# Chunk-selected attention with a gated FFN: units of half a batch for all eight heads, and scores of four heads in row tiles

## The chip, the cores and the metric

The kernel runs on one core of a Trainium2 chip. The metric is the device time in microseconds (us). All comparisons use runs of the same ("fast") state: a run more than 1.5% above the fastest of the same kernel is left out, also from the medians quoted. The kernel before takes 394.27 us (median of 4 runs, 393.13 to 394.62).

Names of the engines in the profile: PE is the matrix engine, PEld its weight loads, DVE the vector engine, ACT the scalar engine, POOL the general engine that also issues the weights' transfers here, and SP the engine that issues the other transfers. PSUM is the memory into which the matmuls of these kernels write, in banks. A row tile is a product that takes only 32 or 64 of the 128 rows of PE, a column tile one that takes only some of its columns; several of them can run side by side.

## The reference

Four batches, eight heads, 768 positions, 64 features per head. Keys lie in 24 chunks of 32. For each query an upper bound of each chunk's scores is computed, and only keys in the six chunks with the largest bounds take part in the attention. The attention's output goes through an FFN with a sigmoid gate (512 to 1536 to 512).

```
k_min, k_max = min and max of the keys of each chunk of 32
ub = sum(maximum(q * k_min, q * k_max), -1)          # per query and chunk
ub = where(causal by chunk, ub, -1e9)
top_chunks = argsort(ub)[..., -6:]
scores = q @ k.T / 8, -1e9 where the chunk isn't chosen or the key is later
attn = softmax(scores) @ v
x = attn, heads side by side                        # 3072 x 512
out = (sigmoid(x @ w_gate) * (x @ w_val)) @ w_out
```

The choice of chunks compares bounds, so these are kept in fp32. Scores, values and FFN use fp16 operands.

## The kernel before

A group is four heads of one batch; there are eight groups. A group's keys are loaded twice, by rows and by chunks (`kc`). The mask of a query is appended to its 64 features as 32 further rows, and so one matmul of 96 rows gives the masked scores of a head. The bounds are one product of 128 rows per head: `[max; -min]` of the chunks against `[relu(q); relu(-q)]`.

```python
nc.sync.dma_start(d["kc"], k[b, h0:h0 + 4].rearrange("h (c s) d -> (h c) s d", s=CH))
...
def chunk_bounds(g):                       # two reduces of 96 x 2048, strided
    nc.vector.tensor_reduce(kmm[:, 0:64], kv, AX.X, ALU.max)
    nc.vector.tensor_reduce(kmm[:, 64:128], kv, AX.X, ALU.min, negate=True)
...
def bounds(g):
    for x in range(2):
        for h in range(4):                 # K = 128, four heads in four column tiles
            nc.tensor.matmul(ps[32 * h:32 * h + 32, x, 0:hw], kcat[g % 2][:, h, :],
                             d[("qcat", h)][:, hw * x:hw * x + hw], start=True, stop=True)
...
def score(g, h, x):                        # one head, one PSUM bank
    hk, hq = headK[4 * (g % 2) + h], headQ[4 * (g % 2) + h]      # [96, 768] each
    ...
    for (jb, i0, w) in banks[x]:
        nc.tensor.matmul(ps[:, o:o + w], hk[:, 128 * jb:128 * jb + 128], hq[:, i0:i0 + w],
                         start=True, stop=True)
        o += w
    nc.scalar.activation(at[:, b0:b0 + n], ps, AF.Exp, scale=scale)
...
def ffn_tasks(b):                          # the FFN waits for a whole batch
    for t0 in range(0, S, TCH):            # two halves of 384 tokens
        ...  12 gate and value products, then 3 outputs
```

The attention of group g, the preparation of group g+1 and the FFN of the batch before are interleaved. The layer that records the kernel reorders each engine's instructions by its own estimate of time, so the built order differs from the source; and each engine then takes its own list in order (e13 below shows PE waiting 5 us for that).

The softmax here doesn't subtract the row's maximum and nothing guards it: scores larger than these inputs give would overflow.

## Time and profile before

| before (profiled span 393.6 us) | |
|---|---|
| PE busy | 320.2 us (81%) |
| first matmul of an FFN output | 136.6 us |
| a batch in the steady part | 82.7 us |
| FFN of the last batch, alone at the end | about 47 us |

First the page of the kernel before: the span, the busy time of each engine with its number of instructions, then the busy tenths of PE and its granted clock in forty slices of the span, then a queue with packets, MB and share.

```profile
span 393.6 us, 6906 instructions
PE 320.2 (81%) x2696; PEld 197.2 (50%) x2696; DVE 230.0 (58%) x486; ACT 204.6 (52%) x393; POOL 73.5 (19%) x77
...
PE   1071549287598999799979998799999999999996
PEclk9996557856969999999999999999999999999999
...
q1 hardware_dynamic: 79616, 31.47, 37.3%
```

A slice is 9.8 us. In the first twelve slices PE has gaps and its clock falls to half; from the thirteenth PE is nearly full. So the kernel has two stages with different limits: a start that waits for inputs, DVE and ACT, and a steady part that is bound by PE.

The chain of waits of the kernel before, with start, duration and what ran, shows the steady rhythm by the first output matmuls of each half batch:

```profile
136.57 2.60 PE o_0_0_1471 L296 x12
...
178.90 2.61 PE o_384_0_2048 L296 x12
...
261.58 2.61 PE o_384_0_3203 L296 x12
```

From 178.90 to 261.58 is one batch, 82.7 us.

The timeline of PE of the kernel before, first where scores pass into gate products, then at the bounds (start, duration, line, output<-inputs, sizes; the durations are longer than the steps because matmuls are pipelined, so read the starts):

```profile
232.26 0.39 PE L243 MATMUL sc_0_0_2792<-hq_132,hk_131 96*128 96x128 f16 x4
232.49 0.38 PE L243 MATMUL sc_0_1_2798<-hq_132,hk_131 96*128 96x128 f16 x3
232.71 0.33 PE L281 MATMUL g_384_0_2804<-xT_0_1456,wg_145 128*128 128x384 f16 x1
...
251.93 0.33 PE L287 MATMUL v_384_7_3041<-xT_3_2194,wv_146 128*128 128x384 f16 x1
252.19 0.46 PE L169 MATMUL ubT_3023<-qcat_0_2859,kcat_139 128*32 128x320 f32 x1
...
252.48 0.43 PE L169 MATMUL ubT_3023<-qcat_0_2859,kcat_139 128*32 128x320 f32 x1
```

Four score blocks of 128 queries, mask included, take 232.26 to 232.49: 0.057 us each. A gate matmul of 384 columns takes 0.16. The value matmul at 251.93 hands over to the bounds 0.26 us later, 0.1 us more than its usual step: a change of the tile shape from 128x128 to 128x32 costs about that. Each fp32 product of the bounds shows as two passes.

### The profile page before, as it was taken

The numbers are of one execution on the slowest core, as the hardware profiler recorded it, in microseconds if no ns is written. First come the engines' busy times: TensorE is split into PE (matmuls) and PEld (weight loads), VectorE is DVE, ScalarE is ACT, GpSimd is POOL, SyncE is SP. The second block draws the span as 40 slices with busy tenths as digits, with TensorE's granted clock in tenths as the row PEclk, the third lists the DMA queues.
The fourth block names the chain that finished last, engine by engine and source line by source line (L and its number), as shares of the span: only waits on it lengthen the run. The fifth ranks groups of instructions, "written<-read, shape, count | busy, mean of one in ns | idle before, by whom it ended". The sixth has DMA issues, their size and how long they took to land.

```text
span 393.6 us, 6906 instructions
## 1 busy us (share of the span) xinstructions
PE 320.2 (81%) x2696; PEld 197.2 (50%) x2696; DVE 230.0 (58%) x486; ACT 204.6 (52%) x393; POOL 73.5 (19%) x77
## 2 busy tenths in 40 slices
PE   1071549287598999799979998799999999999996
PEld 0040335164464656455645555465666566565552
DVE  4947629967949745855596658664556544142230
ACT  1150446266576548555556656655876466332331
POOL 4504143232312051003300230011101001000000
PEclk9996557856969999999999999999999999999999
DMA  9999999297920964433615010002000100100102
GB/s 181 217 214 214 208 212 195 66 217 148 214 62 15 226 156 108 101 62 86 155 42 120 28 55 0 2 2 80 2 2 27 55 2 1 55 27 28 54 2 80
DMA packets 84400, 36.62 MB, mean 93 GB/s; under 512 B 75920, under 2 KB 80528, under 8 KB 83600
## 3 DMA queue, kind: packets, MB, share of 16 engines
q1 hardware_dynamic: 79616, 31.47, 37.3%
q0 software_dynamic: 4752, 4.72, 7.2%
q8 instruction: 21, 0.34, 0.4%
q14 instruction: 11, 0.09, 0.1%
HBM read 34.60 MB, written 6.29 MB: 104 GB/s over the span
## 4 chain that ended last, share of the span: by engine, by line
PE 58%; DVE 17%; ACT 8%; issue 6%; SPq 5%; DMA 4%; POOL 1%; ACTq 0%; DVEq 0%; POOLq 0%
SPq L125 5%; DMA k_177<-in_k_dram 3%; DMA kc_151<-in_k_dram 2%; DVE kmm_1096 L140 1%; DVE kmm_209 L140 1%; DVE kmm_721 L141 1%; DVE kmm_1096 L141 1%; DVE kmm_209 L141 1%; PE o_0_0_2626 L296 1%; PE o_0_0_3781 L296 1%; PE o_384_0_3203 L296 1%; PE o_384_0_2048 L296 1%; PE o_0_0_1471 L296 1%; PE o_384_2_4783 L296 1%; PE o_384_1_4298 L296 1%
## 5 line engine op out<-in xcount | busy, mean ns | idle before, releaser
L287 PEld LDWEIGHTS <-wv_146 128*128 128x128 f16 x384 | 37.9, 99 | 28.3 <-issue 4.2
L281 PEld LDWEIGHTS <-wg_145 128*128 128x128 f16 x384 | 35.7, 99 | 23.2 <-issue 6.7
L153 PE MATMUL qT_0_212<-ident_103,q_148 128*128 128x128 f32 x5 | 1.3, 426 | 8.4 <-DMA q_148<-in_q_dram 8.4
L243 PEld LDWEIGHTS <-hk_123 96*128 96x128 f16 x48 | 4.8, 122 | 3.8 <-issue 2.9
L153 PE MATMUL qT_1_227<-ident_103,q_148 128*128 128x128 f32 x5 | 1.3, 427 | 5.9 <-DVE qcat_1_221 L160 5.9
L153 PE MATMUL qT_0_369<-ident_103,q_176 128*128 128x128 f32 x5 | 1.3, 426 | 5.8 <-DMA q_176<-in_q_dram 5.8
L140 DVE TENSOR_REDUCE kmm_1096<-kc_1044 96x64 f32<-96x2048 f32 x1 | 3.7, 3667 | 3.7 <-PE kct_756 L146 3.7
L272 PE MATMUL xps_1_671<-ident_108,xnat_400 128*128 128x128 f16 x6 | 0.8, 307 | 6.1 <-DVE xnat_400 L265 6.1
L140 DVE TENSOR_REDUCE kmm_209<-kc_151 96x64 f32<-96x2048 f32 x1 | 3.6, 3591 | 3.8 <-DMA kc_151<-in_k_dram 3.8
L272 PEld LDWEIGHTS <-xnat_400 128*128 128x128 f16 x24 | 2.1, 120 | 7.2 <-DVE xnat_400 L265 6.9
L243 PEld LDWEIGHTS <-hk_135 96*128 96x128 f16 x48 | 4.3, 109 | 2.4 <-issue 1.1
L290 DVE SCALAR_TENSOR_TENSOR hg_384_0_4595<-gate_384_0_4588,v_384_0_4590 128x384 f16<-128x384 f16 x1 | 0.6, 553 | 8.5 <-PE v_384_0_4590 L287 8.5
L243 PEld LDWEIGHTS <-hk_125 96*128 96x128 f16 x48 | 4.5, 110 | 1.9 <-issue 0.5
L193 PEld LDWEIGHTS <-ap_140 128*128 128x128 f16 x20 | 1.5, 106 | 7.7 <-DVE ap_140 L187 6.1
L264 DVE RECIPROCAL rz_0_423<-pv_0_401 128x6 f32<-128x6 f32 x1 | 0.2, 195 | 8.8 <-PE pv_0_401 L261 8.8
L193 PE MATMUL apT_316<-ident_108,ap_140 128*128 128x128 f16 x5 | 0.7, 309 | 5.7 <-DVE ap_140 L187 5.7
L243 PEld LDWEIGHTS <-hk_131 96*128 96x128 f16 x48 | 4.1, 107 | 2.3 <-issue 1.1
L243 PEld LDWEIGHTS <-hk_133 96*128 96x128 f16 x48 | 4.3, 108 | 1.8 <-issue 0.2
L153 PEld LDWEIGHTS qT_0_212<-ident_103,q_148 128*128 128x128 f32 x5 | 0.9, 220 | 8.3 <-issue 8.3
L140 DVE TENSOR_REDUCE kmm_359<-kc_179 96x64 f32<-96x2048 f32 x1 | 3.6, 3597 | 2.4 <-DMA kc_179<-in_k_dram 2.4
L261 PE MATMUL pv_0_401<-v_141,att_0_335 128*128 128x65 f16 x21 | 1.3, 244 | 4.5 <-POOL att_0_335 L249 4.5
L243 PEld LDWEIGHTS <-hk_127 96*128 96x128 f16 x48 | 4.2, 106 | 1.6 <-issue 0.2
(2400 smaller groups left out, 1201.9 us busy)
## 6 DMA issues: line engine op xcount, KB each, us to landing
wg_145<-in_moe_w_gate_dram POOLq DMA_DIRECT2D x3, 512.0 KB, 9.8
wv_146<-in_moe_w_val_dram POOLq DMA_DIRECT2D x3, 512.0 KB, 7.7
wo_147<-in_moe_w_out_dram POOLq DMA_DIRECT2D x3, 512.0 KB, 12.9
kc_151<-in_k_dram SPq DMA_DIRECT2D x1, 768.0 KB, 5.9
q_148<-in_q_dram SPq DMA_DIRECT2D x4, 192.0 KB, 6.6
k_149<-in_k_dram SPq DMA_DIRECT2D x4, 192.0 KB, 6.5
v_150<-in_v_dram SPq DMA_DIRECT2D x4, 192.0 KB, 7.3
kc_179<-in_k_dram SPq DMA_DIRECT2D x1, 768.0 KB, 17.0
```

What stands on the lines that cost most here:

```text
L125: nc.sync.dma_start(d[n][:, :, h, :], src[b, h0 + h].rearrange("(sb p) d -> p sb d", p=128))
L140: nc.vector.tensor_reduce(kmm[:, 0:64], kv, AX.X, ALU.max)
L141: nc.vector.tensor_reduce(kmm[:, 64:128], kv, AX.X, ALU.min, negate=True)
L153: nc.tensor.transpose(ps[:, 128 * i:128 * i + 128], d["q"][:, i + 1, 2 * pr:2 * pr + 2, :].rearrange("p h d -> p (h d)"), ident32)
L193: nc.tensor.transpose(ps[:, 128 * i:128 * i + 128], apt[g % 2][:, i, :, :].rearrange("p h c -> p (h c)"), ident16)
L243: nc.tensor.matmul(ps[:, o:o + w], hk[:, 128 * jb:128 * jb + 128], hq[:, i0:i0 + w], start=True, stop=True)
L261: nc.tensor.matmul(ps[:, ib, :], at[:, c:c + 128], v16s[g % 2][:, jb, h, :], start=(jb == 0), stop=(jb == ib))
L272: nc.tensor.transpose(ps[:, 128 * ib:128 * ib + 128], xnat[b][:, ib, 128 * c:128 * c + 128], ident16)
L281: nc.tensor.matmul(gp, wg16[:, c, 128 * fb:128 * fb + 128], xT[(b, c)][:, t0:t0 + TCH], start=(c == 0), stop=(c == 3))
L287: nc.tensor.matmul(vp, wv16[:, c, 128 * fb:128 * fb + 128], xT[(b, c)][:, t0:t0 + TCH], start=(c == 0), stop=(c == 3))
L290: nc.vector.scalar_tensor_tensor(hg, gate, 1.0, vp, ALU.add, ALU.mult)
L296: nc.tensor.matmul(op, hgl[(b, t0, fc)][:, 128 * tb:128 * tb + 128], wo16[:, fc, :], start=(fc == 0), stop=(fc == NFB - 1))
```

## The change

The intent was to start the FFN earlier and to take work off DVE, ACT, POOL and the queues. A unit is now half the positions of one batch for all eight heads. Keys and queries are transposed in fp32 straight from their loads; the chunks' max and min are reduced from those transposes in PSUM, and so the second load of the keys goes. Bounds become products of 64 rows, positive and negative part one after the other. Scores take four heads at once into four PSUM banks: for each block, first four mask matmuls of 32 rows in four row tiles, then four key matmuls of 64 rows, two heads at a time in two row tiles.

```diff
-    pff: 3 PSUM buffers, psc: 3, pbig: 1 (two banks)
+    pff: 3 PSUM buffers, psc: 4, ppr: 1 (one bank)     # abridged
...
+    def keys_t(u, p, pool):
+        ps = pool.tile([128, T], F32, tag="ps", name=f"kT_{u.name}_{p}")
+        for x in range(HB):
+            nc.tensor.transpose(ps[:, 128 * x:128 * x + 128],
+                                u.k[:, x, 2 * p:2 * p + 2, :].rearrange("p h d -> p (h d)"), ident32)
+        ...
+        for e, op in enumerate((ALU.max, ALU.min)):
+            nc.vector.tensor_reduce(out=kmx[u.b % 2][:, p, e, c0:c0 + T // CH], in_=pv, op=op, axis=AX.X)
+        nc.scalar.copy(k16[u.b][:, p, u.rows], ps)
...
+    def bounds(u):
+        ps = [(ppr, psc)[j].tile(...) for j in range(2)]
+        for e in range(2):
+            for i in range(4):
+                for j in range(2):
+                    c = i ^ j
+                    h = 4 * j + c
+                    r = 64 * (h % 2)
+                    nc.tensor.matmul(ps[j][32 * c:32 * c + 32, 0:n], kmx[u.b % 2][r:r + 64, h // 2, e, :],
+                                     u.qs[r:r + 64, h // 2, e, s0:T], start=(e == 0), stop=(e == 1))
...
+    def score(u, heads, x):
+        for (jb, i0, w) in u.banks[x]:
+            plain = i0 + w <= 128
+            if not plain:
+                for h in heads:
+                    r = 32 * (h % 4)
+                    nc.tensor.matmul(ps[h][:, o:o + w], epat[r:r + 32, 128 * jb:128 * jb + 128],
+                                     u.mask[r:r + 32, h // 4, i:i + w], start=True, stop=False)
+            for h in heads:
+                r = 64 * (h % 2)
+                nc.tensor.matmul(ps[h][:, o:o + w], k16[u.b][r:r + 64, h // 2, 128 * jb:128 * jb + 128],
+                                 u.q16[r:r + 64, h // 2, i:i + w], start=plain, stop=True)
+            o += w
...
+    for c, t in prep_tasks(units[0], [ppr, psc]):      # unit 0: two pools for its transposes
         t()
+    load(units[1])
     for i in range(3):
         load_w(i)
...
+            prep = prep_tasks(units[i + 1], [ppr])      # every later unit: one buffer
```

## The prediction

> **What bounds the kernel now.** The windows view shows two regimes. From about 120 us to the end PE is busy 17 to 20 us of every 20. In the timeline of PE each group (four heads of one batch) repeats every 41.3 us (first FFN output matmul 178.90, 220.25, 261.58 in the chain of waits). By starts of matmuls a group holds 24 gate and value products at 0.65 us and three outputs at 2.6, 23.4 us; scores 1.15 per head, 4.6; values 0.65 per head, 2.6; transposes (fp32 0.108 each, fp16 0.056) 4; bounds 1.2. That is 36 us of matmul and 5 of stalls. Before 112 us there is no such filler: PE is busy about half the time, the queues move about 215 GB/s, the clock falls to 0.5, DVE does two strided reduces of 3.6 us per group, and the first FFN starts in earnest at about 111 us. At the end the FFN of a whole batch (two halves of 23.4 us) runs alone.
>
> **What the change removes.** The third load of keys (0.79 MB per group), both 3.6 us reduces per group, the fp16 casts of q and k (POOL 1.47 us each). Half a batch (2.4 MB) is enough to start the FFN.
>
> **What it adds.** Per unit, 24 fp32 transposes (2.6 us of PE, against 1.1 + 1.3 before); eight reduces of 128x384 from PSUM, estimated at 0.45 us from the 128x384 DVE operations (0.55). Scores: heads pair in the K=64 product and four share the K=32 mask, ideally three quarters of the time. But weight loads grow from 11 per head to some 29, and row-tile modes alternate twice per block. The Trainium skill, "TensorEngine Tiling (Array Packing)", Key Properties, says that changing the tiling mode drains TensorE; this trace shows about 0.1 us of gap into and out of the column-tiled bounds. Switching some 56 times per batch would cost 5.6 us. My estimate: scores 8 to 14 us per batch against 9.2 now. So steady PE work is 71 to 77 us per batch, against 72: no gain there. ACT and DVE get lighter, off the path.
>
> **Sum.** DMA issue and landing put unit 0's keys at about 8 us, queries 13; its masks at about 25; its attention, with preparation of unit 1 (whose loads share the queues with the weights), ends at 45 to 50 us, when the FFN starts in earnest. After that: FFN 8 x 23.5 = 188 us; remaining attention work about 97; stalls about 3 per unit, 22 in all. 47 + 188 + 97 + 22 = 354. I predict 354 us, 8 in 10 between 337 and 377. Chances: faster by over 2% 0.94, same 0.04, slower 0.02.
>
> **What in the profile would show it.** First run of gate matmuls near 47 us instead of 111 (timeline). PE nearly full from 50 us (slices). Tail with FFN alone about 24 us, not 47. A pair of units takes 79 to 85 us, hardly less than two groups (82.6). Per batch, score matmuls occupy 8 to 14 us by their starts, with gaps where mask and key products alternate. DMA total falls by 6.3 MB.
>
> **What would make it wrong.** Scores of four heads take all four PSUM buffers: four exponentials (0.5 us apart) must end before the next round; preparation has a single PSUM buffer for every transpose, so the chain transpose, two reduces, transpose may stall PE (370 to 390). Mode switches costing more than 0.1 us. Or later first loads, behind the weights. Faster if row tiles overlap fully and switching is free: about 337.

## The result, and the profile after

Ratios here are the mean time of one kernel's fast runs over that of the other's in the same rounds, so they are not quite the ratio of the medians quoted.

| | before | after |
|---|---|---|
| time, median (range), us | 394.27 (393.13 to 394.62) | 424.69 (423.74 to 427.13) |
| ratio to before (95%) | | 1.0786 (1.0734 to 1.0839) |
| profiled span | 393.6 | 422.3 |
| first FFN output matmul | 136.6 | 117.1 |
| a batch in the steady part | 82.7 | 90.5 |

The changed kernel is 7.9% slower. The prediction had said 354 us and faster.

The page of the kernel after, the same lines:

```profile
span 422.3 us, 8095 instructions
PE 376.1 (89%) x3280; PEld 199.4 (47%) x3280; DVE 175.1 (41%) x527; ACT 183.2 (43%) x401; POOL 55.5 (13%) x94
...
PE   0267668899999999999999999999999999999996
PEclk9997558689999999899999999999999999999999
...
q1 hardware_dynamic: 78336, 25.17, 27.5%
```

The intent worked everywhere but on PE. The queue moved 6.3 MB less, DVE lost 55 us of work, ACT 21 and POOL 18, and PE is at least nine tenths busy from the ninth slice on. Yet PE is busy 56 us longer. Its chain of waits:

```profile
85.45 0.75 PE g_0a_745 L291 x2
...
117.07 2.70 PE o_0a_1209 L306 x12
...
208.98 2.70 PE o_1a_2522 L306 x12
...
299.48 2.70 PE o_2a_3835 L306 x12
```

The steady batch went from 82.7 us to 91.9 and 90.5. The earlier first output is also less of a gain than it looks: at 136.6 us the kernel before had done the attention of about one and a half batches, the changed one at 117.1 us that of one, since the FFN of a unit is interleaved with the attention of the next.

**Where PE's time went.** The most useful reading of the two traces is this sum over the whole span. For each matmul I take the time from its start to the start of the next one, less the idle time between its modelled end and that next start, and add by kind. (Modelled ends make idle and work a little uncertain against each other; their sum is exact.)

| us of PE, whole span | before | after | difference |
|---|---|---|---|
| scores | 48.2 | 76.9 | +28.7 |
| bounds | 13.0 | 28.0 | +15.0 |
| transposes of queries, keys and chunk bounds | 27.7 | 33.3 | +5.6 |
| FFN | 194.4 | 199.5 | +5.1 |
| values and the other transposes | 36.5 | 37.9 | +1.4 |
| idle between matmuls | 61.4 | 38.5 | -22.9 |
| ahead of the first matmul and after the last one's start | 12.3 | 8.1 | -4.2 |
| span | 393.6 | 422.3 | +28.7 |

So the change bought 27 us of idle time and paid 56 us of work on the engine that binds the steady part. Two terms, scores and bounds, are 44 of the 56. The timeline of PE after shows the reason for the first. All four heads at once, one block of 128 queries and then one of 256:

```profile
211.83 0.23 PE L244 MATMUL sc_1b_3_2558<-mask_1b,epat 32*128 32x128 f16 x1
...
212.00 0.23 PE L248 MATMUL sc_1b_3_2558<-q_1b,k_1_713 64*128 64x128 f16 x1
212.00 0.23 PE L248 MATMUL sc_1b_3_2559<-q_1b,k_1_713 64*128 64x128 f16 x1
212.06 0.22 PE L248 MATMUL sc_1b_3_2560<-q_1b,k_1_713 64*128 64x128 f16 x1
212.07 0.22 PE L248 MATMUL sc_1b_3_2561<-q_1b,k_1_713 64*128 64x128 f16 x1
212.22 0.28 PE L244 MATMUL sc_1b_3_2558<-mask_1b,epat 32*128 32x256 f16 x1
...
212.22 0.28 PE L244 MATMUL sc_1b_3_2561<-mask_1b,epat 32*128 32x256 f16 x1
212.43 0.28 PE L248 MATMUL sc_1b_3_2558<-q_1b,k_1_713 64*128 64x256 f16 x1
```

The four masks start together and so do the pairs of heads: row tiles do run at once, as the Trainium skill says ("TensorE: Matmul & The Clock Gate", Part 3, where four row tiles of 512 columns are given as 3.07 times as fast). But the steps are long. Within the keys the second pair starts 0.06 us after the first; from there to the masks it is 0.15. For the 128-query block four heads take 0.17 us of masks and 0.22 us of keys, 0.39 in all; the kernel before needs 4 x 0.057 = 0.23 for the same scores with their masks. Over the batch the step at a change between 64 and 32 rows is 0.15 to 0.16 us for 128 columns, where 0.057 is usual, and 0.20 to 0.21 for 256 columns, where 0.11 is usual: about 0.10 us of loss per change. The Trainium skill ("TensorEngine Tiling (Array Packing)", Key Properties) says why a loss is to be expected: changing the tiling mode drains the engine. There are 107 changes between unlike tile shapes per batch (96 rows counted with 128), so about 11 us; before there were 4. Of the 107, 56 lie between 32 and 64 rows, 43 between score tiles and work on all 128 rows, such as the FFN, that the built order puts between the blocks, and 8 at the bounds. The steps that count as scores hold 78 of them. By estimate, the 17.0 us of scores per batch without 78 x 0.10 would be 9.2, close to the 10.15 of the kernel before: the changes can account for the whole excess.

And the built order often breaks up the sets of four. Of 38 sets of masks per batch (the source has 28) only 19 hold all four heads. Here one head goes alone, the same timeline a little later:

```profile
222.54 0.23 PE L248 MATMUL sc_2a_0_2718<-q_2a,k_2_2026 64*128 64x128 f16 x1
222.70 0.22 PE L244 MATMUL sc_2a_0_2718<-mask_2a,epat 32*128 32x128 f16 x1
222.86 0.23 PE L248 MATMUL sc_2a_0_2718<-q_2a,k_2_2026 64*128 64x128 f16 x1
```

Every matmul changes the mode, 0.16 us a step, and nothing shares it. (The source puts a block's masks ahead of its keys; in the built order of single heads they alternate without end.)

The timeline of PE at the bounds of one upper half:

```profile
241.03 0.84 PE L192 MATMUL ubT_2b_3000<-qs_2b,kmx_144 64*32 64x384 f32 x4
...
242.92 1.48 PE L192 MATMUL ubT_2b_3000<-qs_2b,kmx_144 64*32 64x384 f32 x12
244.34 0.50 PE L291 MATMUL g_1b_3021<-xT_1b,wg_156 128*128 128x384 f16 x2
244.76 1.49 PE L192 MATMUL ubT_2b_2999<-qs_2b,kmx_144 64*32 64x384 f32 x16
246.19 0.50 PE L291 MATMUL g_1b_3021<-xT_1b,wg_156 128*128 128x384 f16 x2
```

The two banks go one after the other, with 16 passes per bank (four passes of the first ran 1.9 us ahead of the rest). The second bank takes 16 passes in 1.43 us, from start to next start: four rounds of four at about 0.36. The product of 64 rows runs at 64x32 places, and there are eight of these (e9 below shows rounds of eight); but with `c = i ^ j; h = 4*j + c; r = 64*(h % 2)` the row half is always that of the column c, so that both banks use the same four places (c % 2, c). With half the rows, twice the products, and still four at a time, the bounds cost more than twice as much (5.9 us per batch against 2.4).

Last the start. The timeline of all engines after, where unit 1's transposes go through their one PSUM buffer, and ahead of that the line of PE on which unit 0's first half waited for its queries (idle time before it and its releaser in brackets):

```profile
22.85 0.47 PE L172 MATMUL qT_0a_190<-ident_118,q_0a 128*128 128x128 f32 x1 [2.36 <-DMA q_0a<-in_q_dram]
...
50.33 0.90 PE L158 MATMUL kT_0b_382<-ident_118,k_0b 128*128 128x128 f32 x3 [1.68 <-ACT k_0_159 L164]
51.27 1.02 DVE L163 TENSOR_REDUCE kmx_144<-kT_0b_382 128x12 f32<-128x384 f32 x2 [1.56 <-PE kT_0b_382 L158]
52.38 0.48 ACT L164 CAST k_0_159<-kT_0b_382 128x384 f16<-128x384 f32 x1 [2.10 <-DVE kmx_144 L163]
52.92 0.90 PE L172 MATMUL qT_0b_391<-ident_118,q_0b 128*128 128x128 f32 x3 [1.68 <-ACT k_0_159 L164]
```

One pair of heads takes 2.59 us from transpose to transpose, and PE works for 0.9 of it. The cast on ACT waits for the reduces on DVE though both only read the tile. The Trainium skill ("PSUM — Partial Sum Buffer", Terms) says that two engines must not use the same bank and the same 32 partitions at once, reads against reads included, which would be why they are kept apart; the wait is seen here (2.10 us idle, ended by DVE), a collision in no run. The windows view after gives the clock in this stretch, beside the DMA share and GB/s in the last columns:

```profile
40.00:60.00 20.00, 12.59 (x58) 5.86 (x58) 6.04 (x12) 8.11 (x18) 4.74 (x8) 0.50 1.07 197
```

PE is busy 12.6 us of 20, at half its clock.

### The profile page after: what moved, and what is told of

Same layout as the page of the kernel before. It is cut to its first block, busy times and chain, and to the rows that moved or that the text cites. A ratio compares the mean times of both kernels' runs of the same rounds, so it can differ in the third digit from the quotient of the medians.

```text
span 422.3 us, 8095 instructions
## 1 busy us (share of the span) xinstructions
PE 376.1 (89%) x3280; PEld 199.4 (47%) x3280; DVE 175.1 (41%) x527; ACT 183.2 (43%) x401; POOL 55.5 (13%) x94
## 2 busy tenths in 40 slices
DMA packets 83125, 30.41 MB, mean 72 GB/s; under 512 B 75408, under 2 KB 80016, under 8 KB 83088
## 4 chain that ended last, share of the span: by engine, by line
PE 71%; ACT 11%; DVE 8%; DMA 3%; issue 3%; SPq 2%; ACTq 0%; DVEq 0%
DMA q_0a<-in_q_dram 3%; SPq L99 2%; PE ubT_0b_464 L192 1%; DVE kmx_144 L163 1%; DVE kmx_150 L163 1%; DVE ap_145 L217 1%; PE o_2a_3835 L306 1%; PE o_1a_2522 L306 1%; PE o_3a_5042 L306 1%; PE o_0a_1209 L306 1%; PE o_3b_5392 L306 1%; PE o_3a_5171 L306 1%; PE o_2a_3910 L306 1%; PE o_3b_5376 L306 1%; PE o_2b_4416 L306 1%
## 5 line engine op out<-in xcount | busy, mean ns | idle before, releaser
L297 PEld LDWEIGHTS <-wv_157 128*128 128x128 f16 x384 | 37.8, 99 | 27.1 <-issue 5.9
L291 PEld LDWEIGHTS <-wg_156 128*128 128x128 f16 x384 | 33.6, 99 | 25.4 <-issue 8.1
L244 PEld LDWEIGHTS <-epat 32*128 32x128 f16 x448 | 15.6, 92 | 29.1 <-issue 21.5
L158 PE MATMUL kT_0a_160<-ident_118,k_0a 128*128 128x128 f32 x3 | 1.4, 466 | 10.6 <-DMA k_0a<-in_k_dram 10.6
L248 PEld LDWEIGHTS <-k_0_159 64*128 64x128 f16 x120 | 5.4, 97 | 8.9 <-issue 6.1
L172 PE MATMUL qT_0a_190<-ident_118,q_0a 128*128 128x128 f32 x3 | 1.4, 457 | 8.9 <-DMA q_0a<-in_q_dram 8.9
L248 PEld LDWEIGHTS <-k_3_3339 64*128 64x128 f16 x120 | 4.3, 94 | 5.1 <-issue 2.4
L248 PEld LDWEIGHTS <-k_1_713 64*128 64x128 f16 x120 | 4.3, 94 | 4.7 <-issue 1.9
L248 PEld LDWEIGHTS <-k_2_2026 64*128 64x128 f16 x120 | 4.3, 94 | 4.6 <-issue 1.8
L163 DVE TENSOR_REDUCE kmx_144<-kT_0a_181 128x12 f32<-128x384 f32 x2 | 1.0, 553 | 9.8 <-PE kT_0a_181 L158 9.8
L192 PE MATMUL ubT_0b_464<-qs_0b,kmx_144 64*32 64x384 f32 x16 | 4.3, 844 | 0.6 <-ACT qs_0b L175 0.6
L225 PEld LDWEIGHTS <-ap_145 128*128 128x128 f16 x20 | 1.1, 97 | 7.5 <-DVE ap_145 L217 7.5
L151 POOL CAST v_146<-v_2a 128x1536 f16<-128x1536 f32 x1 | 1.5, 1465 | 24.5 <-PE pv_0b_1343 L270 24.5
L151 POOL CAST v_152<-v_3a 128x1536 f16<-128x1536 f32 x1 | 1.5, 1465 | 24.5 <-PE pv_1b_2656 L270 24.5
L163 DVE TENSOR_REDUCE kmx_144<-kT_0a_160 128x12 f32<-128x384 f32 x2 | 1.0, 552 | 8.3 <-PE kT_0a_160 L158 8.3
L111 POOL TENSOR_SCALAR_AFFINE_SELECT epat<-epat 32x768 f16<-32x768 f16 x4 | 4.0, 990 | 0.2
## 6 DMA issues: line engine op xcount, KB each, us to landing
wv_157<-in_moe_w_val_dram POOLq DMA_DIRECT2D x3, 512.0 KB, 10.7
```

What stands on the lines that cost most here:

```text
L111: nc.gpsimd.affine_select(out=epat[32 * h:32 * h + 32], in_=epat[32 * h:32 * h + 32], compare_op=ALU.not_equal, fill=NEG, base=0, pattern= ...
L151: nc.gpsimd.tensor_copy(v16s[u.b % 2][:, u.qa:u.qb, :, 0:D], u.v)
L163: nc.vector.tensor_reduce(out=kmx[u.b % 2][:, p, e, c0:c0 + T // CH], in_=pv, op=op, axis=AX.X)
L172: nc.tensor.transpose(ps[:, 128 * x:128 * x + 128], u.q[:, x, 2 * p:2 * p + 2, :].rearrange("p h d -> p (h d)"), ident32)
L192: nc.tensor.matmul(ps[j][32 * c:32 * c + 32, 0:n], kmx[u.b % 2][r:r + 64, h // 2, e, :], u.qs[r:r + 64, h // 2, e, s0:T], start=(e == 0), ...
L244: nc.tensor.matmul(ps[h][:, o:o + w], epat[r:r + 32, 128 * jb:128 * jb + 128], u.mask[r:r + 32, h // 4, i:i + w], start=True, stop=False)
```

## The experiments

Theory at the outset: (a) the drains between 64-row and 32-row tiles and the doubled bounds make the steady part longer; (b) late queries and the one PSUM buffer keep the start long. Rivals: PE's extra time is inherent in four heads sharing four PSUM banks (waiting for the exponentials); or the start is bound by its half clock. Each experiment edits the changed kernel. In the cuts of edits below, a line in plain words stands for the code that it sums up. First output means the first matmul of the first FFN output, period the time of one batch between like outputs.

### Steady part: the scores

**e1_snake**: fewer mode changes, same matmuls. Within a bank the order alternates, keys then masks for one block, masks then keys for the next.

```diff
-            if not plain: masks of all heads;  then keys of all heads
+            for part in ("k",) if plain else (("m", "k") if masks_next else ("k", "m")):
+                ...
+            if not plain:
+                masks_next = not masks_next
```

> Same work as the changed kernel (422 us), but within a PSUM bank the order is keys-masks, masks-keys, keys-masks, so that about 18 of the 107 changes of tile height per batch go away. Theory (each change between the K=32 masks, the K=64 keys and full-array work costs about 0.11 us of PE): scores occupy about 2 us less per batch, 415 to 419 us in all. Rival (the cost is the extra weight loads, or the waits of four heads for four PSUM buffers): within 0.5% of the changed kernel. Result stays correct.

Measured: 417.35 us, ratio 1.063 (1.0578 to 1.0681). Changes fell from 107 to 86 per batch, scores from 17.0 to 15.1 us, the period to 89.4. The estimate 21 x 0.10 = 2.1 us per batch against 1.9 measured: the loss per change holds, and since every weight load stayed, the number of weight loads is not what costs. Idle time rose from 2.7 to 3.6 us, so that the period fell by 1.1 only.

**e2_k96_four**: the 96-row scores of before (mask appended to the features), four heads at once as in the change. To fit the memory, attention buffers 8 to 7 and FFN buffers 24 to 22.

```diff
-   masks: K=32 in four row tiles; keys: K=64 in two row tiles
+                nc.tensor.matmul(ps[h][:, o:o + w], headK[u.b % 2][h][:, 128 * jb:128 * jb + 128],
+                                 headQ[u.half][h][:, i:i + w], start=True, stop=True)
```

> Undoes the row tiles alone: scores are again one K=96 product per block as in the kernel before, everything else (units, fp32 transposes, bounds, four heads at once) as in the changed kernel; attention buffers 7 instead of 8 and FFN buffers 22 instead of 24 for room. Theory (row tiles cost 17.0 us of PE per batch against 10.2 for K=96): about 6.5 us per batch less, 394 to 400 us. Rival (waits of four heads for four PSUM buffers, not the row tiles): within 1% of 424.

Measured: 402.92 us, 1.0255 (1.0219 to 1.029). The timeline of PE:

```profile
203.31 0.82 PE L245 MATMUL sc_1b<-hq,hk 96*128 96x128 f16 x8
203.97 0.81 PE L303 MATMUL o_1a<-wo,hg_1a 128*128 128x512 f16 x3
```

Eight blocks of queries with their masks take 0.66 us, and there is no mode change inside. Scores fell to 10.7 us per batch (before: 10.15), the changes to 12, the period to 84.9. Four heads at once stayed, so the four banks are not what made the scores long. This one part is worth 22 of the 30 us by the medians. The expected 394 to 400 us was missed by 3: the scores fell by 6.3 us as expected, but the FFN took 1.4 us per batch more and the period fell by 5.6.

**e3_k96_one**: the same, with one head at a time.

```diff
-HEADS_AT_ONCE = 4
+HEADS_AT_ONCE = 1      # and e2's scores
```

> As e2, but one head at a time. Theory: PE is busy in the steady stage, the order of heads is hidden there, so it equals e2 within 1% (394 to 400), perhaps 1 to 3 us less at the start. Rival (four at once is what costs): e3 is faster than e2 by 10 us or more.

Measured: 406.25 us, 1.0321 (1.0282 to 1.036). The period is shorter, 83.6, but the first output later, 119.3 against 113.8. So four at once costs a little in the steady part and helps here at the start; neither is the main cause. It lies within 1% of e2, as expected, but not in the range of 394 to 400.

### Steady part: the bounds

**e6_bounds_k128**: positive and negative parts stacked to 128 rows per head as before, so half as many products; DVE and ACT work grows.

```diff
-    for e in range(2): two accumulating products of 64 rows per head
+        for j in range(2):
+            for c in range(4):
+                nc.tensor.matmul(ps[j][32 * c:32 * c + 32, 0:n], kmx[u.b % 2][:, 4 * j + c, :],
+                                 u.qs[:, 4 * j + c, s0:T], start=True, stop=True)
```

> The changed kernel with bounds computed as in the kernel before: positive and negative parts stacked to K=128 per head, so half as many fp32 products; for that half-width copies on ACT and DVE come back. Theory (bounds take 5.9 us of PE per batch, because each fp32 product runs as two passes of which I counted one, and K=64 doubles their number): bounds fall to 2.5 to 3 us per batch, total 409 to 413 us. Rival (ACT and DVE, or the chain through the one preparation buffer, now bound): 418 to 428.

Measured: 435.26 us, 1.1066 (1.1026 to 1.1107). A miss: 11 us slower than the change itself. The bounds fell only from 5.9 to 4.9 us per batch, since the products of the upper halves came in pieces as their inputs arrived; idle time rose from 2.7 to 4.4, scores from 17.0 to 17.8, DVE from 175 to 215 us, and the first output came at 125.0. The theory that stacking is the cheap way back fell.

**e9_bounds_eight**: the products of 64 rows stay, but bank 1's heads are laid so that the eight products use all eight 64x32 places. Both banks come from the four-buffer pool.

```diff
-        ps = [(ppr, psc)[j].tile(...) for j in range(2)]
+        ps = [psc.tile(...) for j in range(2)]
-                    c = i ^ j
-                    h = 4 * j + c
+                    c = i
+                    h = 4 * j + (c ^ j)
...
-                    r = 32 * (h % 4)
+                    r = 32 * ((h % 4) ^ (h // 4))
```

> The changed kernel with its K=64, M=32 bounds on eight places of the array instead of four: in the second bank the heads of a pair change columns, so that even heads stand on columns 32 to 63 and 96 to 127 there, and both banks come from the scores' four buffers, so they can be issued by turns. As many matmuls as before. Theory (the bounds' 5.9 us of PE per batch are mostly serial passes of four at a time): 3 to 4 us per batch, total 411 to 416 us. Rival (fp32 passes don't overlap beyond four, or what is freed is lost to waits, as in e6): 419 to 426.

Measured: 409.99 us (fast runs 409.38 to 413.66; one slow run of 417.56 left out), 1.0471 (1.0402 to 1.0541). The timeline of PE, first at the bounds of a lower half, then of an upper one:

```profile
193.14 1.09 PE L192 MATMUL ubT_2a<-qs_2a,kmx 64*32 64x256 f32 x32
194.16 0.28 PE L244 MATMUL sc_1b<-mask_1b,epat 32*128 32x256 f16 x2
...
229.79 1.51 PE L192 MATMUL ubT_2b<-qs_2b,kmx 64*32 64x384 f32 x30
231.24 0.82 PE L291 MATMUL g_1b<-xT_1b,wg 128*128 128x384 f16 x4
```

In the upper half 30 passes take 1.45 us (the other two ran 1.9 us earlier), where the change took 1.43 us for a bank of 16. Bounds fell from 5.9 to 3.2 us per batch, scores stayed (17.3). The lower half shows that the places did this and not the other pool: there the change too runs both banks in one stretch, with passes of both banks in one round, but never more than four at once, and its 32 passes take 2.32 us (205.02 to 207.34) against 1.03 here. So eight places do run at once, and the change's doubled bounds came from its placing of the heads. The first output also came 9 us earlier (108.1); whether the places or the other pool did that this run does not tell apart.

### The start

**e4_weights_late**: the weights' transfers wait for unit 0's queries, by a column written first.

```diff
+    for t in (wg16, wv16):
+        for i in range(3):
+            nc.gpsimd.tensor_copy(t[:, 0, 512 * i:512 * i + 1], units[0].q[:, 2, 0, 0:1])
```

> The changed kernel, but each weight load also waits for the last part of the first unit's queries, by one written column that the load overwrites. Theory (weight loads issued at 1.4 to 9.4 us hold up the first queries, which land at 22.9 us): queries land at 13 to 15 us, masks of unit 0 are ready 8 us earlier, and 5 to 9 us of it reach the end: 415 to 419 us. Rival (the single PSUM buffer of the preparation of unit 1 bounds the start anyway, and later weights hold up the first FFN): 422 to 426.

Measured: 420.41 us, 1.0691 (1.066 to 1.0721), short of the expected 415 to 419. The queries were all there at 14.5 us instead of 22.9, unit 0's last mask transposes ran at 30.4 instead of 38.7, and yet the first output came only 3.7 us earlier (113.4). Late queries are a cause, but eight microseconds at the masks are mostly lost again in what follows.

**e5_prep_buffers**: unit 1's transposes over three PSUM buffers instead of one (two of them the FFN's, not needed yet).

```diff
-            prep = prep_tasks(units[i + 1], [ppr])
+            prep = prep_tasks(units[i + 1], [(ppr, 'ps'), (pff, 'ff'), (pff, 'ff')] if i == 0 else [(ppr, 'ps')])
```

> The changed kernel, but the eight transposes of unit 1 rotate over three PSUM buffers (the preparation's one and two of the FFN's, idle then) instead of one. Theory (from 39 to 78 us the start is bound by a chain of about 2.6 us per pair through the one buffer: transposes, two reduces, cast, next transposes): FFN matmuls start 8 to 12 us earlier and the whole takes 411 to 416 us. Rival (the halved clock and the in-order engines bound it): within 3 us of the changed kernel's 422.

Measured: 415.24 us, 1.0553 (1.051 to 1.0595), from three fast runs; the profiled run, slow (670.89 us), is not used, so there is no account of where the time came from.

**e13_start_both**: e4 and e5 together.

> The changed kernel, row tiles and all, with e4's late weights and e5's three buffers together; gives also a readable trace of the start, as e5's profile fell in a slow state. Theory (the start is two delays in series, the late first queries and then the one-buffer chain of unit 1's preparation, so that e4's 8 us of earlier masks come out once the chain is loosened): more than the sum of e4 and e5 (4 + 9), 406 to 410 us, first output matmul at 101 to 105 us instead of 117. Rival (the two overlap): 412 to 416.

Measured: 421.75 us, 1.0705 (1.0671 to 1.074), first output 116.5. A miss: the two gains do not add, they nearly cancel. The timeline of PE:

```profile
41.19 0.45 PE L172 MATMUL qT_0b<-ident,q_0b 128*128 128x128 f32 x1 [5.01 <-DMA q_0b<-in_q_dram]
41.42 0.42 PE L225 MATMUL apT_0a<-ident,ap 128*128 128x128 f16 x2
...
47.19 0.47 PE L172 MATMUL qT_0b<-ident,q_0b 128*128 128x128 f32 x1 [5.34 <-DMA q_0b<-in_q_dram]
```

With free buffers the recording layer drew unit 1's transposes ahead of unit 0's mask transposes. PE takes its list in order, so it waited twice, 5.01 and 5.34 us, for loads that unit 0 does not need, and the mask transposes, done at 30.4 in e4, ran from 41.4 to 50.5. From there to the first output it was 66 us, against 83 in e4: the work of unit 1 that had moved ahead of the masks no longer came after them, which fits that the two gains nearly cancel.

**e14_warm**: useless matmuls of 128x384 between the tasks of unit 0, into the FFN's idle PSUM, to keep the clock up. Nothing else changes.

```diff
+    def warm():
+        d = pff.tile([128, T], F32, tag="ff", name=f"warm_{nwarm[0]}")
+        for _ in range(4):
+            nc.tensor.matmul(d, ident16, epat[:, 0:T], start=True, stop=True)
...
+        if i == 0:
+            a = [y for x in a for y in (x, (0.0, warm))]
```

> The changed kernel with matmuls of no use, four of 128x384 into the idle FFN buffers after each task of the preparation of unit 0 and of its attention, to hold the granted clock up from 25 to 80 us, where it is 0.5 to 0.8. Theory (half clock doubles the PE part of the chain, about 0.45 us in each of 12 transposes plus the scores): FFN starts 4 to 8 us earlier, 414 to 418 us. Rival (the chain is DVE, ACT and semaphores; the clock does not matter, the extra matmuls get in the way): 422 to 430.

Measured: 414.66 us, 1.0536 (1.0515 to 1.0556), first output 108.8. The windows view and the timeline of PE:

```profile
40.00:60.00 20.00, 19.52 (x165) 9.59 (x163) 7.53 (x15) 9.01 (x22) 3.35 (x5) 1.00 1.18 208
```

```profile
42.06 0.55 PE L158 MATMUL kT_0b<-ident,k_0b 128*128 128x128 f32 x3
...
44.28 0.55 PE L158 MATMUL kT_0b<-ident,k_0b 128*128 128x128 f32 x3
```

The clock holds at 1.00, and the eighth gate or value product of the FFN starts at 75.1 us instead of 81.7. This agrees with the Trainium skill ("TensorE: Matmul & The Clock Gate", Part 1), by which the throttled clock is the default and activity releases it. So the half clock is part of a long start, some 8 us; but at full clock a pair of heads still takes 2.2 us (42.06 to 44.28), because DVE and ACT, not PE, fill most of that chain. The rival explains a part, not the whole.

### Together

**e7_all_four** and **e8_all_one** put e2 (or e3), e4, e5 and e6 together; they were in the same job as e6, before its result was known.

> All that helped at once: K=96 scores with four heads at once, bounds at K=128, late weights, three buffers for unit 1. If the parts add up: 403 - 4 - 10 - 12 = 377 us, faster than the kernel before by 4%; 372 to 384. If the parts overlap (the same start time counted twice): 384 to 392.

> As e7 but one head at a time: 374 to 386 us if the parts add up; within 1% of e7.

Measured: 412.19 us, 1.0482 (1.0454 to 1.0509), and 406.05 us, 1.0313 (1.0282 to 1.0344). Both miss. In e7 the bounds took 6.0 us per batch, idle time rose to 5.2, and DVE to 246 us.

**e10_three_parts_four** and **e11_three_parts_one** are the same without the stacked bounds.

> e2 (K=96 scores, four heads at once) with late weights and three buffers for unit 1, without the K=128 bounds. If e6's loss was the bounds' own: 403 - 4 - 9 = 390 us, level with the kernel before; 387 to 394.

> As e10, but one head at a time. If the order of heads stays hidden behind a busy PE, as e3 against e2: 387 to 395 us, within 1% of e10.

Measured: 394.15 us (the mean of two fast runs, 391.95 and 396.35; two slow ones of 397.9 left out), 1.0022 (0.9945 to 1.0099), and 389.5 us, 0.9903 (0.9871 to 0.9935): both the same as before within 2%. Against e7 and e8 they differ only by the bounds: 18.0 and 16.5 us less, so stacking costs about that much in this setting too. The periods are those of e2 and e3 (84.9 and 83.6); the rest came from the start, with first outputs at 103.7 and 104.3.

**e12_eight_one**: e11 with e9's bounds.

> e11 with the bounds of e9: 3 us per batch less if the passes overlap, 376 to 384 us, which would beat the kernel before by 3 to 4%; otherwise as e11.

Measured: 385.28 us, 0.9805 (0.9766 to 0.9843), unclear at 2% and just above the expected 376 to 384. The period fell from 83.6 to 82.0, the first output did not move (104.0).

**e15_best_warm**: e12 with e14's useless matmuls.

> e12, the fastest so far, with the same useless matmuls in the first unit: 379 to 383 us if the clock matters at the start, 384 to 390 if not.

Measured: 388.59 us, 0.9881 (0.9853 to 0.9909), first output 108.1. Slower than e12, so the clock did not help here. Why was not shown: the filler may stand in the way where fewer waits are left, but the built order changed too (unit 0's last mask transposes ran at 35.1 us instead of 49.7).

**e16_best_early_weights** is e12 without e4's edit; **e17_best_one_buffer** is e12 without e5's.

> e12 (K=96 scores, one head at a time, bounds on eight places, late weights, three buffers) without the late weights. Theory from e13 (with three buffers and late weights the in-order PE takes unit 1's transposes ahead of unit 0's masks and waits there for inputs that the weights now hold up, so the two changes cancel): this is as fast as e12 or faster, 380 to 386 us. Rival (what cancelled in e13 is special to the row tiles' order): 388 to 394.

> e12 without the three buffers, late weights kept. Same theory: masks of unit 0 come early again, as in e4, and this loses less than the 9 us of e5: 384 to 390. Rival: 392 to 396, the buffers are what helps.

Measured: e16 383.3 us (382.07 to 383.59), 0.9729 (0.97 to 0.9757); e17 386.74 us, 0.9816 (0.9789 to 0.9844). Late weights cost 2 us here by the medians; three buffers gain 1.5 by the medians, with overlapping intervals. The page of e16:

```profile
span 381.6 us, 7361 instructions
PE 332.4 (87%) x2832; PEld 200.1 (52%) x2832; DVE 202.0 (53%) x615; ACT 213.2 (56%) x449; POOL 56.5 (15%) x94
```

e16 is the fastest kernel, 2.7% faster than before and about 10% faster than the change as it came. It is the only one that is faster than before by over 2% in its whole interval. It keeps the half-batch units, the fp32 transposes and the bounds from PSUM, has the bounds on eight places and three buffers for unit 1, and takes back the row tiles of the scores and the four heads at once. In the sum used above it has 44.5 us of scores, 24.1 of bounds and 41.4 of idle time, 332.0 of work in all: 12 us more work than before, and 24 us less time without work.

## Why the prediction was wrong

The prediction was 354 us, and the profiled span was 422: 68 us more. By its own sum, "47 + 188 + 97 + 22", 35 of these lie before the FFN flows and 33 after it.

**The start, +35 us.** The step that failed is "its attention, with preparation of unit 1 [...] ends at 45 to 50 us, when the FFN starts in earnest". The first gate matmul started at 70.8 us, the eighth gate or value matmul at 81.7, which is taken here as the start in earnest. The prediction had counted PE's own work and the first loads. The runs showed three things in its place. First, the queries landed at 22.9 us instead of 13, behind weights that POOL had issued from 1.4 us on (e4: 8 us at the masks, 3.7 at the first output). Second, the preparation of unit 1 is a chain through one PSUM buffer in which DVE and ACT read one after the other, 2.59 us per pair, while PE works for 0.9. The prediction named this buffer under "what would make it wrong" but gave the chain no time in its sum; its estimate of 0.45 us for a reduce is near the 0.51 measured, and the sum of three such operations in a row, beside the transposes, is what it lacked. Third, the clock was 0.50 from 40 to 60 us (e14: about 8 us). These three overlap and their gains do not add, as e13 shows; how they share the 35 us is not settled.

**The steady part, +33 us.** The step that failed is "So steady PE work is 71 to 77 us per batch, against 72". Measured were 87.8 us (the period of 90.5 less 2.7 idle), against 74.6 before (82.7 less 8.1). By terms:

- *Scores, "8 to 14 us per batch"*: 17.0 were measured. The mechanism, drains at mode changes, was right, and "0.1 us" was right too (about 0.10). The count was wrong: "some 56 times per batch" was 107. Between masks and keys there were indeed 56 (partly luck: the built order broke up sets of four and put FFN work between others); the 43 changes between score tiles and full-row work, which that order also makes, and the 8 at the bounds had not been counted. For blocks of 128 queries the two changes cost about 0.20 us per four heads, and the whole 96-row form takes 0.23 with the masks in it, so that there was nothing left to gain. e2 took the row tiles back and kept everything else: scores 10.7, time 22 us less.
- *Bounds, no term of their own*: 5.9 us per batch against 2.4 before. The prediction did not see that the eight heads use only four of the eight places. e9 puts them on eight: 3.2.
- *Transposes*: the "2.6 us of PE" per unit was 3.1; they cost 1.1 us per batch more than before.

Two periods of 91.9 and 90.5 us, against the predicted 79 to 85 (82 in the middle), are 18 of the 33. The other 15 lie after them, where the third period took 84.5 us with no further unit to prepare at its end, and ahead of them, between 82 us and the first output at 117, where the clock was still 0.80 from 80 to 100 us. These 15 were not taken apart.

**What was right.** Stalls: "about 3 per unit" was 2.7 per batch, even less. PE nearly full in the steady part: yes. The last FFN alone takes about 23 us (predicted 24). DMA traffic fell by 6.2 MB (36.62 to 30.41; predicted 6.3). DVE, ACT and POOL got lighter, off the path, and for that reason it helped the steady part little. The rival "four banks wait for four exponentials" was in the prediction's risks and did not come true: with the four banks kept, e2's idle time is 2.5 us per batch.

**What stays open.** How late weights and more buffers act on each other: each gains alone, together they cancel on the changed kernel (e13), and in the best version late weights cost 2 us. The one mechanism shown is the order that the recording layer chooses (e13's waits for loads). e5's own gain has no readable trace. Also open are the source of e9's earlier first output, and e10's scatter of 6 us between its own runs (two of the four count as slow).

## What to carry to other kernels

When PE is full, first add up what a change costs PE, for the whole span and by kind: less idle time and lighter other engines could not pay here for 56 us of added PE work. Row tiles paid here where many products of one shape follow each other (the bounds on eight places), while alternating shapes block by block cost more than the tiles saved, and folding a 32-row mask into a 64-row product (96 rows) did the same work with no change of shape. For tiles that should run at once, write down the (row, column) place of each product and check in the trace how many passes share a round; and check edits that each gain alone once more together, because the built order may change under them.

## What the Trainium skill lacked or had wrong

- "TensorEngine Tiling (Array Packing)", Key Properties: it says that a mode change drains the engine but gives no figure. Here it cost about 0.10 us per change between 32-row and 64-row tiles (steps of 0.15 to 0.16 us for 128 columns where 0.057 is usual); there were 107 changes of all kinds per batch. e1, with the same weight loads and 21 changes fewer, saved 0.09 us per change, so the loss goes with the change; whether it is the drain or weights that load only after it was not separated.
- "TensorE: Matmul & The Clock Gate", Part 3: the 3.07 times for four row tiles is for 512 columns, and nothing is said there of a change of mode. In this kernel four masks of 128 columns took 0.17 us with the change, where four matmuls of 128 columns one after the other are about 0.23 (4 x 0.057, an estimate): 1.4 times. That four row tiles start together agrees.
- "TensorEngine Tiling (Array Packing)", Tiling Modes: it lists eight places for 64x32 and speaks of no data type. Here eight fp32 products did run at once (32 passes of 256 columns in 1.03 us, against 2.32 on four places).
- "FP8 and Floating Point Precision", TensorE Precision Notes: it gives four passes for a true fp32 product. The trace shows two matmul records per product, each with a step of 0.27 us for 320 columns where fp16 takes 0.16 for 384, so about twice the time per column: the total agrees, the number of records is not in that page.
- "PSUM — Partial Sum Buffer", Terms: it says that two readers must be kept apart, but not what this costs in a chain of transposes: here reduces of 1.02 us and a cast of 0.48 us ran one after the other, 2.59 us per pair of heads in one buffer, and 2.2 us even at full clock.
